# Small loads of the folded tables in another order, their users five and three steps later, and folds of batch 2 in other steps

## The chip, the cores and the metric

The kernel runs on one core of a Trainium2 chip. The metric is the device time of one execution in microseconds. Every time below is from runs on the chip or from the profile of one execution.

A core has engines that run side by side, each through its own list of instructions in order: PE (matrix multiplication into PSUM), DVE and POOL (element by element), ACT (functions and copies), and SP, which in this kernel only issues DMAs. An instruction that must wait for another engine or for a DMA holds up everything behind it on its own engine.

## The reference

A Fourier transform over sequence and features, of which the real part is kept, and then a gated feed-forward block:

```python
def _attn_ref(x):                                  # x: 8 x 3008 x 256
    X = np.fft.fft(x, axis=1)
    X = np.fft.fft(X, axis=2)
    return X.real.astype(np.float32)

def _moe_ref(x, w_gate, w_val, w_out):             # x: 24064 x 256, d_ff 1536
    gate = 1.0 / (1.0 + np.exp(-(x @ w_gate)))
    val = x @ w_val
    return (gate * val @ w_out).astype(np.float32)
```

## The kernel before

**Steps.** After a start-up, one loop runs 576 steps: 8 batches of 6 chunks of 12 steps (`i0` = 12, `per` = 72). A chunk is 252 output rows and their mirror images; a step is one slice of 128 of the 1536 hidden features. In step `i` PE multiplies `pk` (`front_a`) and `qk` (`front_b`) of the chunk into a PSUM bank, ACT and DVE make gate times value of step `i - 1` out of its bank (`gate_a`, `gate_b`), and PE multiplies older results with the output weights (`back`). Three PSUM banks rotate. A bank is started by ACT (`seed`, L851), which for step `i` must wait until the bank's previous use, step `i - 3`, is over: its last reader is `gate_b(i - 3)` (DVE L897), which stands in pass `i - 2` of the loop. `front_a` of step `i` waits for its `seed`.

**POOL.** Every three steps are a group. After the second and the third step of a group POOL makes seven and six sums of blocks of the hidden activations (L903, tile `sf`), which PE reads some three steps later (`po<-sf`).

**Closing a chunk.** `back` of the last group copies PSUM into the tile `c` in two steps, 3 and 4 after the start of the next chunk (`i % 12` of 3 and 4), and queues 24 small jobs in `later`: sums on `c` (DVE L987), transposes into `os` (DVE L995) and the stores (SP L1011, L1015). Each step takes two or three of them.

**Side work by hand.** Work for the next batch is put into steps by number: `at(i, f)` runs `f` at the end of step `i`; `gap[i]` runs it on DVE inside `gate_b`, just ahead of L897, in place of one job of `later`; `mid` puts matmuls between two steps. There is no scheduler: every engine has its instructions in the order in which these calls make them.

**Folds.** `fold_ops(b, 2)` gives the folds of batch `b` on POOL: six `point` (L550) and two small `first` (L554), six `across` (L563), three `feat` (L557, L558, L560, a trio), then seven more. `later_folds(b, s0)`, where `s0` is the first step of the batch before, spreads the first 17 over steps. For batch 2, `s0` is 72. In `gap[s0 + 18]` and on, `turn` (DVE L621) multiplies the folded data by tangents; the first two `turn` read what the second trio wrote, the next two need the third trio.

**Folded tables.** From batch 2 on a folded table is used. `table_rows` and `quarter_load` (SP L308) bring it into tiles named `st` in the profile. `quarter_small(i)` (eight DMAs each, one number per row and column) brings `self` (i = 0), `other` (i = 1; both L319) and `angle` (i = 2, L315), in steps 78, 79 and 80 (`per + 6 + i`). `quarter_ops` works on them: `turns` makes tangents of `angle` (L336 to L338), `eight` (L357) makes sums of the table, `ratios` uses `self` and `other` (L341 to L343), `cross` uses the table (L347 to L350). Five of these go into `gap`, in the order of the steps 83 to 87: `turns`, `eight(0)`, `eight(1)`, `ratios`, `cross`. `xr` copies for batch 3 (L156 to L169) go out on SP in steps 75 to 79 and 87 on.

**SP.** All these DMAs, the stores of the output and the loads of `ek` (L839) share SP's one queue, in order.

Of the kernel before, what the change touches and what calls it, by code (L numbers as in the profile page):

```python
# [81 lines left out]
def kernel(  # L82
# [216 lines left out]
    def quarter_src(g, par, t, cols):  # L299
        return (stab[0:TB, t, par:NQ:2, cols], rtab[par * TB : (par + 1) * TB, t, :, cols])[g]  # L300
# [10 lines left out]
    def quarter_small(i):  # L311
        for g, par, lo in TILES:
            if i == 2:
                for t in range(2):
                    nc.sync.dma_start(out=TAB["angle"][lo : lo + TB, t * N3 : (t + 1) * N3],  # L315
                                      in_=quarter_src(g, par, t, NE))
            else:
                for h, col in enumerate((0, NE)):
                    nc.sync.dma_start(out=TAB[("self", "other")[i]][lo : lo + TB, h * N3 : (h + 1) * N3],  # L319
                                      in_=quarter_src(g ^ i, par, 0, col))  # L320
# [772 lines left out]
    per = NFT * len(chunks)  # L1093
    side, mid, gap = {}, {}, {}

    def at(i, *fs):
        side.setdefault(i, []).extend(fs)
# [18 lines left out]
    i0 = NFT  # L1116
# [40 lines left out]
        at(per + 2 + i, lambda i=i: quarter_load(i // 2, i % 2))  # L1157

    for i in range(3):
        at(per + 6 + i, lambda i=i: quarter_small(i))  # L1160

    def make_tables():
        clear, between, sums, copies = quarter_ops()
        at(per + 7, clear)
        for i, f in zip((11, 12, 13, 14, 15), between, strict=True):
            gap[per + i] = [f]
        for i, f in zip((10, 19), sums):
            at(per + i, f)
        for i, f in zip((21, 23, 17, 19, 25, 27), copies, strict=True):
            at(per + i, f)  # L1170
    at(per + 5, make_tables)

    def later_folds(b, s0):

        ops = fold_ops(b, 2)
        slots = [i for i in range(s0 - (3 if b == 2 else i0), s0 + i0 + 5) if i % i0 < 5 or i < s0 and b == 2]
        for i, f in enumerate(ops[0:17]):
            at(slots[i * len(slots) // 17], f)
        for i, f in zip((24, 25, 26, 27, 28, 36, 37), ops[17:], strict=True):
            at(s0 + i, f)  # L1180
        for i, f in enumerate(TURN.pop(b)):
            gap[s0 + 18 + i] = [f]
        swaps, last, first = MORE.pop(b)
        at(s0 + 24, swaps[1])
        at(s0 + 39, swaps[0])
        for i, f in enumerate(first):
            gap[s0 + 28 + i] = [f]
        for i, f in enumerate(last):
            gap[s0 + 43 + i] = [f]
# [6 lines left out]
    for b in range(2, B):  # L1196
        s0 = (b - 1) * per
        at(s0 - 4 if b == 2 else s0 - i0 - 1, lambda b=b, s0=s0: later_folds(b, s0))
        at(s0 + 3 * i0 + 2, lambda b=b: seq_start(b))
        for blk in range(2):  # L1200
            mid[s0 + (4 - blk) * i0 + 5] = lambda b=b, blk=blk: quarter(b, blk)
        at(s0 + 4 * i0 + 5, lambda b=b, s0=s0: later_ends(b, s0))
        if b < B - 1:
            at(s0 + 4 * i0 + 6, lambda b=b: load_x(b + 1))
            for i, f in enumerate(mirror_x(b + 1)):
                at(list(calm(s0))[i // 2], f)
# [3 lines left out]
    for i in range(count):  # L1210
# [14 lines left out]
        between = gap.pop(i, [])  # L1225
        if not between and later and i < count - 8:
            between = [later.pop(0)]
# [75 lines left out]
```

## Time and profile before

| | us |
|---|---|
| median of 3 runs | 1921.85 (1921.27 to 1922.58) |
| the profiled execution | 1923.08 |
| its span, first to last instruction | 1921.3 |
| PE busy | 1900.5 (99%) |
| DVE busy | 1517.0 (79%) |
| ACT busy | 1353.3 (70%) |
| POOL busy | 1545.7 (80%) |

The page has, for each engine, the time in which it did something and that time's share of the span. PE is the engine that is nearly always busy. An average hides single stretches, so the other views matter: the waits (who waited for whom, total, times, longest), the timeline of an engine (start, length, engine, line, operation, output <- input, shape, count, and in brackets the idle time before it with what ended it), and tables of chosen stretches (busy time of each engine, instructions in brackets, then the granted clock of PE, the share of the DMA engines and GB/s). In a timeline, instructions of one line that follow each other are merged into one row, with their number at its end.

The mean granted clock of PE over the span is 0.997 of full speed.

The same lines of code in different batches can be told apart by time: batch 1's steps begin at 285.93 us (step 72), and steps there are about 3.1 us apart.

### The profile page before, as it was taken

What the parts mean: (1) busy time and instruction counts of PE and PEld (TensorE: products, weight loads), DVE (VectorE), ACT (ScalarE), POOL (GpSimd) and SP (SyncE); (2) the same over time, 40 slices, a digit from 0 to 9 for tenths busy, and PEclk for the clock granted to TensorE, in tenths of its full rate; (3) what the DMA queues carried; (4) which work ended last, traced back from release to release, by engine and by line L of the source; (5) the groups of instructions that cost most, each with busy time, mean ns of one, the idle gap of its engine ahead of it and who ended that gap; (6) DMA issues with size and microseconds to landing.
All of it is one profiled execution on the core that took longest, in us unless ns stands there. A gap on an engine that the chain in (4) does not pass through costs nothing.

```text
span 1921.3 us, 35824 instructions
## 1 busy us (share of the span) xinstructions
PE 1900.5 (99%) x11740; PEld 1760.8 (92%) x11740; DVE 1517.0 (79%) x3351; ACT 1353.3 (70%) x3219; POOL 1545.7 (80%) x2742
## 2 busy tenths in 40 slices
PE   8999998999999999999999999999999999999999
PEld 5799997999999999999999999999999999999998
DVE  7677875977978789787788877988788787976775
ACT  4876765777777777777777777777767777777775
POOL 2489967996999879997799877999789996877770
PEclk9999999999999999999999999999999999999999
DMA  8353234222023121221212123112120120011011
GB/s 313 110 97 72 65 105 96 64 52 79 16 48 73 34 80 21 63 54 31 86 34 60 39 38 87 39 47 50 34 80 14 31 45 15 15 23 19 15 17 30
DMA packets 198833, 110.05 MB, mean 57 GB/s; under 512 B 139269, under 2 KB 189168, under 8 KB 196856
## 3 DMA queue, kind: packets, MB, share of 16 engines
q1 hardware_dynamic: 198070, 107.25, 23.4%
q8 instruction: 94, 1.54, 0.3%
q14 instruction: 91, 0.75, 0.1%
q10 hardware_dynamic: 546, 0.51, 0.1%
q0 software_dynamic: 32, 0.00, 0.0%
HBM read 73.56 MB, written 47.87 MB: 63 GB/s over the span
## 4 chain that ended last, share of the span: by engine, by line
PE 95%; DMA 2%; SPq 1%; ACT 1%; DVE 0%; issue 0%; ACTq 0%; DVEq 0%
PE pf L134 50%; PE po L134 42%; PE sum L134 2%; DMA xr<-in_xf_dram 1%; DMA wf<-in_moe_w_out_dram 1%; SPq L433 1%; PE ps L134 1%; PE ev L134 0%; DMA st<-rtab 0%; SPq L221 0%; DMA raw<-in_moe_w_val_dram 0%; SPq L308 0%; PE pe L134 0%; SPq L164 0%; DVE z L881 0%
## 5 line engine op out<-in xcount | busy, mean ns | idle before, releaser
L903 POOL TENSOR_TENSOR sf<-h,sf 128x168 f32<-128x168 f32 (+1 forms) x1104 | 618.8, 581 | 71.0 <-DVE h L897 69.1
L903 POOL TENSOR_TENSOR sf<-h 128x168 f32<-128x168 f32 (+1 forms) x920 | 522.3, 587 | 180.0 <-DVE h L897 178.0
L134 PE MATMUL pf<-pk,G 128*128 128x252 f32 (+1 forms) x2304 | 583.6, 376 | 9.6 <-ACT pf L851 9.6
L134 PE MATMUL pf<-qk,G 128*128 128x252 f32 (+1 forms) x2304 | 583.6, 376 | 1.0 <-ACT ae L866 1.0
L851 ACT ACTIVATE pf<-ek,ge 128x252 f32<-128x252 f32 (+1 forms) x1142 | 538.3, 471 | 30.6 <-DVE h L897 10.9
L134 PE MATMUL po<-sf,wf 128*128 128x168 f32 (+1 forms) x2944 | 509.0, 306 | 0.0
L134 PEld LDWEIGHTS pf<-pk,G 128*128 128x128 f32 x2304 | 436.3, 190 | 63.3 <-ACT pf L851 10.6
L866 ACT ACTIVATE ae<-pf 128x504 f32<-128x504 f32 (+1 forms) x576 | 339.4, 589 | 219.5 <-PE pf L134 217.8
L134 PEld LDWEIGHTS po<-sf,wf 128*128 128x128 f32 x2944 | 454.4, 190 | 8.1
L897 DVE TENSOR_TENSOR h<-pf,z 128x252 f32<-128x252 f32 (+1 forms) x576 | 240.7, 418 | 279.3 <-ACT pf L894 276.3
L134 PE MATMUL po<-h,wf 128*128 128x168 f32 (+2 forms) x2584 | 460.9, 307 | 0.0
L987 DVE TENSOR_TENSOR c<-c 128x168 f32<-128x168 f32 (+1 forms) x920 | 451.4, 512 | 3.2
L881 DVE TENSOR_TENSOR z<-ae,pf 128x504 f32<-128x504 f32 (+1 forms) x576 | 385.0, 668 | 81.7 <-ACT h L880 77.5
L134 PEld LDWEIGHTS pf<-qk,G 128*128 128x128 f32 x2304 | 410.5, 190 | 32.7 <-ACT ae L866 2.2
L134 PEld LDWEIGHTS po<-h,wf 128*128 128x128 f32 x2584 | 410.5, 190 | 17.6 <-issue 0.9
L880 ACT ACTIVATE h<-pf 128x252 f32<-128x252 f32 (+1 forms) x576 | 217.4, 377 | 147.3 <-PE pf L134 132.1
L894 ACT ACTIVATE pf<-z 128x252 f32<-128x252 f32 (+1 forms) x576 | 214.2, 372 | 115.1 <-DVE h L893 112.3
L893 DVE TENSOR_TENSOR h<-h,pf 128x252 f32<-128x252 f32 (+1 forms) x576 | 233.3, 405 | 0.0
L903 POOL TENSOR_TENSOR sf<-sf 128x168 f32<-128x168 f32 (+1 forms) x184 | 101.4, 551 | 14.4
L903 POOL TENSOR_TENSOR sf<-sf,h 128x168 f32<-128x168 f32 (+1 forms) x184 | 108.6, 590 | 0.0
L970 ACT COPY c<-po 128x504 f32<-128x504 f32 (+1 forms) x138 | 78.5, 569 | 0.0
L995 DVE STREAM_TRANSPOSE os<-c 128x256 f32<-128x256 f32 x188 | 77.0, 428 | 0.4 <-issue 0.3
(166 smaller groups left out, 883.9 us busy)
## 6 DMA issues: line engine op xcount, KB each, us to landing
x<-xr SPq DMA_DIRECT2D x14, 1536.0 KB
out_dram<-os SPq DMA_DIRECT2D x368, 56.0 KB
xr<-in_xf_dram SPq DMA_DIRECT2D x90, 128.0 KB
x<-x SPq DMA_DIRECT2D x96, 96.0 KB
ek<-ed SPq DMA_DIRECT2D x40, 126.0 KB
xr<-in_xf_dram SPq DMA_DIRECT2D x12, 384.0 KB
out_dram<-os SPq DMA_DIRECT2D x284, 7.0 KB
x<-in_xf_dram SPq DMA_DIRECT2D x3, 1024.0 KB
```

What stands on the lines that cost most here:

```text
L134: nc.tensor.matmul(o, l, r, start=start, stop=stop, skip_group_check=True)
L851: nc.scalar.activation(PF[i][:, g], EK[i // NFT], AF.Copy, scale=ge[:, g, f : f + 1])
L866: nc.scalar.activation(AP[i], PF[i], AF.Copy, scale=2.0)
L880: nc.scalar.activation(H[p][:, fh, 0:n], PF[i][:, 0], AF.Sigmoid)
L881: nc.vector.tensor_tensor(z[:, :, ::-1], AP.pop(i), PF[i], op=ALU.subtract)
L893: nc.vector.tensor_tensor(h[:, fh, 0:n], h[:, fh, 0:n], pf[:, 1], op=ALU.mult)
L894: nc.scalar.activation(pf[:, 0], z[:, 0], AF.Sigmoid)
L897: nc.vector.tensor_tensor(h[:, fh, n:], pf[:, 0], z[:, 1], op=ALU.mult)
L903: nc.gpsimd.tensor_tensor(block(p, dst), block(p, a), block(p, b), op=(ALU.subtract, ALU.add)[op])
L970: (nc.vector.tensor_copy if t == 1 or t == 3 else nc.scalar.copy)(C[0][:, 3 * t * R : 3 * (t + 1) * R], PO[t][:, 0 : 3 * R])
L987: nc.vector.tensor_tensor(t[:, dst * R : (dst + 1) * R], *v, op=(ALU.subtract, ALU.add)[op])
L995: nc.vector.transpose(os_[0][:, s, 0:nb, h, :], t[:, c0 : c0 + nb * TB])
```

## The change

Two places of the hand-made order change; no instruction is added or removed.

1. `quarter_small` is called in the order 2, 0, 1 rather than 0, 1, 2: `angle` in step 78, `self` in 79, `other` in 80. `turns` moves from the gap of step 83 to that of step 88, and `ratios` from 86 to 89. `eight(0)`, `eight(1)` and `cross` stay in 84, 85 and 87.
2. The first 17 folds of batch 2 get steps written out by number. The six `point` and two `first` were in steps 69, 69, 70, 71, 72, 72, 73, 74 and are now in 69, 70, 71, 71, 72, 73, 74, 74 (`first` in 71 and 74, as before). The six `across` were in 75, 75, 76, 84, 85, 85 and are now in 83, 84, 84, 85, 86, 86. The three `feat` were in 86, 87, 88 and are now in 87, 88, 89. The other batches keep theirs.

```diff
     for i in range(3):
-        at(per + 6 + i, lambda i=i: quarter_small(i))
+        at(per + 6 + i, lambda i=i: quarter_small((2, 0, 1)[i]))
 
     def make_tables():
         clear, between, sums, copies = quarter_ops()
         at(per + 7, clear)
-        for i, f in zip((11, 12, 13, 14, 15), between, strict=True):
+        for i, f in zip((16, 12, 13, 17, 15), between, strict=True):
             gap[per + i] = [f]
...
     def later_folds(b, s0):
 
         ops = fold_ops(b, 2)
-        slots = [i for i in range(s0 - (3 if b == 2 else i0), s0 + i0 + 5) if i % i0 < 5 or i < s0 and b == 2]
-        for i, f in enumerate(ops[0:17]):
-            at(slots[i * len(slots) // 17], f)
+        calm_ = [i for i in range(s0 - i0, s0 + i0 + 5) if i % i0 < 5]
+        slots = [calm_[i * len(calm_) // 17] for i in range(17)]
+        if b == 2:
+            slots = [s0 + i for i in (-3, -2, -1, -1, 0, 1, 2, 2, 11, 12, 12, 13, 14, 14, 15, 16, 17)]
+        for i, f in zip(slots, ops):
+            at(i, f)
```

A step that has work in its `gap` takes its jobs of `later` behind `gate_b` instead, so those of steps 83, 86, 88 and 89 change places with the moved work; their number per step stays.

## The prediction

> **What bounds the kernel now.** I read the waits first, then PE's timeline around the longest of them, then the other engines' timelines there. PE is busy 1900.5 of 1921.3 us, so only the places where it stands still can be won, and the waits name one large one:
>
> ```profile
> DVE st L336 <- DMA st<-rtab: 12.2, 1, 12.2
> PE pf L134 <- ACT pf L851: 9.6, 1, 9.6
> ```
>
> One DVE instruction waits 12.2 us for small loads; one PE matmul waits 9.6 us for the ACT instruction that starts its PSUM bank. I call "step i" the pass of the main loop that begins on PE with the four matmuls `pf<-pk` of i; steps are 3.12 us apart wherever nothing is late (321.56 to 324.69). PE's timeline (start, length, engine, line, what, count, idle before):
>
> ```profile
> 307.26 1.12 PE L134 MATMUL pf<-qk,G 128*128 128x252 f32 x4 [0.31 <-ACT ae L866]
> 308.21 1.04 PE L134 MATMUL pf<-pk,G 128*128 128x252 f32 x4
> ...
> 311.21 1.12 PE L134 MATMUL pf<-qk,G 128*128 128x252 f32 x4 [0.54 <-ACT ae L866]
> 312.17 1.04 PE L134 MATMUL pf<-pk,G 128*128 128x252 f32 x4
> ...
> 324.69 1.01 PE L134 MATMUL pf<-pk,G 128*128 128x252 f32 x4
> ...
> 337.54 2.05 PE L134 MATMUL pf<-pk,G 128*128 128x252 f32 x4 [9.57 <-ACT pf L851]
> ...
> 342.51 1.01 PE L134 MATMUL pf<-pk,G 128*128 128x252 f32 x4
> ```
>
> Steps 79, 80, 84, 85 and 86 start at 308.21, 312.17, 324.69, 337.54 and 342.51. Step 85 comes 12.85 us after 84 instead of 3.12 (9.73 lost), 86 comes 4.97 after 85 (1.85 lost); 80 comes 3.96 after 79 (0.83 lost), and 79 3.70 after 78 at 304.51 (0.58 lost). The 1.85 us are the clock, in the table of stretches (the column before the DMA share is the granted clock):
>
> ```profile
> 328.00:330.80 2.80, 0.00 (x0) 0.00 (x0) 0.00 (x0) 0.00 (x0) 0.00 (x0) 1.00 0.11 14
> 330.90:341.10 10.20, 3.56 (x11) 3.21 (x12) 5.46 (x15) 3.06 (x7) 4.49 (x8) 0.50 0.27 46
> ```
>
> PE ended its last matmul at 327.97; some 2.9 us later the clock fell to 0.50, and stayed there 10.2 us, 3.56 of them busy. DVE:
>
> ```profile
> 306.80 2.25 DVE L987 TENSOR_TENSOR c<-c 128x164 f32<-128x164 f32 x2
> ...
> 322.77 0.41 DVE L893 TENSOR_TENSOR h<-h,pf 128x252 f32<-128x252 f32 x1
> 335.38 0.18 DVE L336 RECIPROCAL st<-st 128x3 f32<-128x3 f32 x1 [12.20 <-DMA st<-rtab]
> ...
> 357.50 0.78 DVE L621 SCALAR_TENSOR_TENSOR x<-x,st 128x256 f32<-128x256 f32 x1
> ```
>
> L336 stands in step 83 in front of L897, which ends step 83's use of a PSUM bank; L851 refills that bank for step 85. SP shows why it waits: its loads go out one after another, and `angle` (L315) is the last group.
>
> ```profile
> 316.34 2.19 SPq L319 DMA_DIRECT2D st<-in_stab_dram x4
> ...
> 331.96 2.30 SPq L315 DMA_DIRECT2D st<-rtab x4
> ```
>
> POOL has the folds:
>
> ```profile
> 304.87 3.99 POOL L563 TENSOR_TENSOR x<-x 128x512 f32<-128x512 f32 x3
> ...
> 343.41 3.74 POOL L563 TENSOR_TENSOR x<-x 128x512 f32<-128x512 f32 x3
> ...
> 356.55 0.72 POOL L560 TENSOR_TENSOR x<-x 128x254 f32<-128x254 f32 x1
> ```
>
> **The change, part by part.**
>
> *The loads.* Three groups of eight DMAs swap places on SP: `angle` takes the place that begins at 316.34, and the `self` and `other` groups move back by one, `other` to the place 330.03 to 334.27. Two pairs of `xr` copies keep their places between them; bytes and count are the same, so SP is free at the same time. The last landing released DVE at 335.35, 5.3 us after the first issue of its group (330.03). By that span `angle`, last issued at 322.08 in its new place, lands by 327.4 even if all 5.3 us follow the last issue; its use, now in step 88, stands where DVE is at 322.77 + 0.41 + 5 x 3.12 = 338.8: cover 11 us. `other` lands near 335.35; its use L342 is now in step 89, at 341.9, or 341.1 after the 0.8 us won below: cover 5.7 us. L357, which in the trace ran after the wait (338.2), now comes at step 84 near 325.5; its table loads were issued by 314.92, and the longest of that kind in the chain of waits landed 5.54 us after issue, so by 320.5. I cost all three waits at nothing. If a cover went, PE would lose the DVE wait less about 1.6 us (the bank's slack: L897 ended at 358.61 in step 90, its bank was needed at 361.26, and refilling takes 1.07, from 336.47 to 337.54). So -9.73 for the wait and -1.85 for the half clock: **-11.58**.
>
> *The three folds taken out of steps 75 and 76.* The L987 pair at 306.80 takes 2.25 us beside L563, and ends when that ends; step 80's 0.83 us follow from it: **-0.83**. The 0.58 of step 79 follow from an earlier pair (302.06, 3.04 us) that stood behind POOL's own sums until 304.87, and these stay: the sums end no sooner, since one L550 and the small L554 move ahead of the last six. Bounds -0.83 to -1.41; I take the first.
>
> *Where the folds go.* Steps 83 to 86 now carry six L563 (three before, in 84 and 85), and the three trios L557, L558, L560 move from steps 86, 87, 88 to 87, 88, 89. Let T0 be the end of step 83's L897, which releases POOL (336.47). From there POOL had no idle time until 358.86. The first L621 (step 90) needs the second trio, done at 356.55 + 0.72 = 357.27 = T0 + 20.8; DVE came at 357.50, 0.2 us later: no wait, and no room. Now three more L563, 3.74 / 3 = 1.25 each, stand in front of it: done at T0 + 24.55. L621 then holds up L897 behind it on DVE (357.50 to 358.61: 1.11) and the refill (1.07): step 92 starts at T0 + 26.7. Undisturbed, T0 would lie 0.15 after step 84's start (L894 of step 83 ended at 324.38, L897 takes 0.42 and a gap of 0.04), step 92 at T0 + 25.0 - 0.15 = 24.85. So PE waits **+1.9** at step 92. The third trio moves behind step 89's seven sums (358.82 to 362.90), to about T0 + 30.2; its reader (step 92) comes at 27.5 on the old rhythm, and with the 3.4 us by which DVE is late by then hardly waits. DVE runs these steps with little to spare, so I add **+0.3** for a second small wait at steps 93 or 94. POOL's sums of step 90 would be late too: PE reads the second at 366.38 (third `po<-sf` pair of step 93), POOL had it at 363.99; 3.75 later on the T0 scale it is short by 1.3, which the 1.9 at step 92 covers.
>
> The blocking seen at 306.80 can return, since the added folds lie beside L357 and L987: L987 takes 0.32 alone (at 309.88) and the pair there took 2.25. I count none of it separately: each such block is at most one L563 long (1.25), within the bank's slack of 1.6, and before L621 DVE waits 3.4 us anyway. Bounds for the moved folds together: 0 (POOL finds 3.75 us that it didn't use) to +2.9 (below the clock's fall).
>
> [...]
>
> *Ratios and tangents on DVE.* The same six instructions, in steps 88 and 89 rather than 83 and 86; L343 took 1.20 beside L563 and may again. They precede L621, so they lie within its wait: 0.
>
> Sum: -11.58 - 0.83 + 1.9 + 0.3 = -10.2. The profiled execution took 1923.08 us (span 1921.3 and 1.8 around it): 1912.9. The median of the runs is 1.23 lower: **1911.6**.
>
> **The rivals.**
>
> *No new wait.* POOL absorbs the folds: 1921.85 - 12.4 = 1909.4, or 1908.9 with step 79's loss gone. For it: three L563 fewer ahead of T0. Against: POOL idled at T0 already, so room before it is of no use after it, and it was full for 22 us.
>
> *The clock falls.* If the new wait reaches 2.9 us, the clock halves, and 10.2 us at half speed cost 5.1: 1909.4 + 2.9 + 5.1 = 1917.4. Against: 1.9 is 1.0 short, and 0.54 us at 311.21 did nothing to the clock.
>
> [...]
>
> *Slower.* One mechanism, POOL's lateness, hits twice: L621 waits at step 90 and again at step 92 (third trio), each long enough for the clock to fall. Price 2 x (2.9 + 5.1) = 16.0: 1909.4 + 16.0 = 1925.4. It decides where POOL is over 1 us later than reckoned at both. Against: at half clock PE leaves POOL 5 us, which fills the second wait.
>
> *The wait only moves.* Landings could slip with the `xr` copies between them, so that DVE waits at L342: it would need some 19 us of slip to eat the gain, and SP had sent everything by 334.27. Time about 1921.
>
> **How the numbers follow.** Forecast 0.62, no new wait 0.19, clock falls 0.10, slower 0.04, wait moves 0.05. About 0.2% (3.8 us) is what a measurement can tell from no change. The first two are faster, the third by 4.4 us mostly so: faster 0.91, same 0.05, slower 0.04. Range 1908.6 to 1916: from step 79's loss gone to a wait of 2.9 with part of a clock fall; the clock's full price and the last two rivals stay out.
>
> **What would show it.** Right: no idle before L336, L341 or L342; L315 ahead of both L319 groups; clock 1.00 from 324 to 400; the step after 311 on time while 307.26's 0.31 stays; a POOL wait of 1 to 3 us before the first L621, and PE idle once by 1 to 3 us about 25 us after step 84. Wrong: any DMA among DVE's waits after 300; L621 without a wait; PE waiting on `po<-sf`; a second stretch at 0.50.

## The result, and the profile after

| | before | after |
|---|---|---|
| median, us (5 runs each) | 1921.41 (1921.11 to 1922.58) | 1912.46 (1912.02 to 1912.84) |
| the profiled execution, us | 1923.08 | 1912.46 |
| its span, us | 1921.3 | 1910.7 |
| mean granted clock | 0.997 | 1.000 |

The ratio of the times is 0.9952, with a 95% interval of 0.9937 to 0.9967: faster by about 9 us. The forecast was 1911.6.

A measure used from here on is **PE's loss**: for each step from 79 to 108, the distance of its first `pf<-pk` matmul from that of the step before, less the undisturbed 3.125 us, summed over the steps that come more than 0.05 us late. Before it was 12.98 us (0.58 at step 79, 0.83 at 80, 9.73 at 85, 1.84 at 86). After it is 2.63: 0.61 at step 91, 1.04 at 92, 0.57 at 93 and 0.41 in small pieces up to 108. The difference, 10.35, is nearly the whole change of the span, 10.6. The span less the loss is between 1907.8 and 1908.7 us in all 14 profiles of this document, so losses can be compared from chip to chip within about half a us.

The waits of the kernel after (who waited for whom: total, times, longest). These are all the waits of PE's matmuls for ACT and the one wait of DVE's L621 for POOL; the 12.2 us of L336 are gone, and no DMA is among DVE's waits after 300 us:

```profile
PE pf L134 <- ACT ae L866: 0.8, 3, 0.3
DVE x L621 <- POOL x L560: 0.5, 1, 0.5
PE pf L134 <- ACT pf L851: 0.3, 1, 0.3
```

PE's timeline after, the first matmuls of steps 79, 80 and of 90 to 94:

```profile
307.85 1.01 PE L134 MATMUL pf<-pk,G 128*128 128x252 f32 x4
310.97 1.01 PE L134 MATMUL pf<-pk,G 128*128 128x252 f32 x4
...
342.22 1.01 PE L134 MATMUL pf<-pk,G 128*128 128x252 f32 x4
345.96 1.03 PE L134 MATMUL pf<-pk,G 128*128 128x252 f32 x4
350.12 1.12 PE L134 MATMUL pf<-pk,G 128*128 128x252 f32 x4 [0.29 <-ACT pf L851]
353.81 1.12 PE L134 MATMUL pf<-pk,G 128*128 128x252 f32 x4
357.04 1.01 PE L134 MATMUL pf<-pk,G 128*128 128x252 f32 x4
```

Steps 79 and 80 are 3.12 apart, and so is every step up to step 90 at 342.22. Then come 3.74, 4.16, 3.69 and 3.23. The loss is read from these starts, not from the brackets, since in the records the matmuls ahead end some 0.15 us behind the next start where nothing waits (308.86 against 308.69). The stretch in which the clock had been 0.50 is full (PE first, the granted clock before the DMA share):

```profile
330.90:341.10 10.20, 10.20 (x62) 9.66 (x62) 9.12 (x20) 8.69 (x20) 10.12 (x15) 1.00 0.44 66
```

SP sends `angle` first and `other` last:

```profile
316.54 1.89 SPq L315 DMA_DIRECT2D st<-in_stab_dram x4
...
331.12 1.87 SPq L319 DMA_DIRECT2D st<-in_stab_dram x4
```

DVE and POOL in the steps where the new loss arises:

```profile
304.96 1.24 DVE L987 TENSOR_TENSOR c<-c 128x164 f32<-128x164 f32 x2
...
339.01 1.27 DVE L338 TENSOR_SCALAR st<-st 128x3 f32<-128x3 f32 x1
...
343.32 0.38 DVE L342 TENSOR_TENSOR st<-st 128x6 f32<-128x6 f32 x1
...
347.98 0.74 DVE L621 SCALAR_TENSOR_TENSOR x<-x,st 128x256 f32<-128x256 f32 x1 [0.51 <-POOL x L560]
```

```profile
331.73 3.75 POOL L563 TENSOR_TENSOR x<-x 128x512 f32<-128x512 f32 x3
...
338.97 2.53 POOL L563 TENSOR_TENSOR x<-x 128x512 f32<-128x512 f32 x2
...
347.22 0.72 POOL L560 TENSOR_TENSOR x<-x 128x254 f32<-128x254 f32 x1
```

The second trio ends at 347.94 and releases the first L621 at 347.98. But DVE waited only 0.51 us for it: it had come late itself. From 336.7 to 347.4 it has hardly any idle time, and the moved work lies in there (L338, which works on 3 numbers per row, took 1.27 us beside an L563). So two engines arrive late together, and the profile alone doesn't tell which of them PE pays for. That is what most experiments ask.

### The profile page after: what moved, and what is told of

It reads as the page before. It is cut to its first block, busy times and chain, and to the rows that moved or that the text cites. A ratio compares the mean times of both kernels' runs of the same rounds, so it can differ in the third digit from the quotient of the medians.

```text
span 1910.7 us, 35839 instructions
## 1 busy us (share of the span) xinstructions
PE 1899.5 (99%) x11740; PEld 1759.9 (92%) x11740; DVE 1513.2 (79%) x3351; ACT 1351.7 (71%) x3219; POOL 1543.8 (81%) x2742
## 4 chain that ended last, share of the span: by engine, by line
PE 97%; DMA 1%; DVE 1%; ACT 1%; POOL 1%; issue 0%; SPq 0%; ACTq 0%; DVEq 0%; POOLq 0%
PE pf L134 51%; PE po L134 43%; PE sum L134 2%; DMA x<-in_xf_dram 1%; PE ps L134 1%; PE ev L134 1%; DMA raw<-in_moe_w_val_dram 0%; PE od L134 0%; POOL sf L903 0%; DVE z L881 0%; POOL x L563 0%; ACT ae L866 0%; PE pe L134 0%; DVE wf L451 0%; ACT wl L533 0%
## 5 line engine op out<-in xcount | busy, mean ns | idle before, releaser
L897 DVE TENSOR_TENSOR h<-pf,z 128x252 f32<-128x252 f32 (+1 forms) x576 | 240.7, 418 | 283.7 <-ACT pf L894 280.8
L987 DVE TENSOR_TENSOR c<-c 128x168 f32<-128x168 f32 (+1 forms) x920 | 443.1, 504 | 3.2
L893 DVE TENSOR_TENSOR h<-h,pf 128x252 f32<-128x252 f32 (+1 forms) x576 | 233.2, 405 | 0.0
```

The source lines that it names most:

```text
L893: nc.vector.tensor_tensor(h[:, fh, 0:n], h[:, fh, 0:n], pf[:, 1], op=ALU.mult)
L897: nc.vector.tensor_tensor(h[:, fh, n:], pf[:, 0], z[:, 1], op=ALU.mult)
L987: nc.vector.tensor_tensor(t[:, dst * R : (dst + 1) * R], *v, op=(ALU.subtract, ALU.add)[op])
```

## The experiments

Each edit is against the kernel after unless it says otherwise. Each comparison has its own runs of the kernel before, on the same chip; their medians were 1922.43 (old folds, folds alone, old load order, DVE relieved), 1923.07 (before again, load order alone, users elsewhere, two folds early), 1922.10 (both relieved, after again) and 1922.53 (the last two).

**Old folds.** The kernel after with the fold steps of before:

```diff
-        calm_ = [i for i in range(s0 - i0, s0 + i0 + 5) if i % i0 < 5]
-        slots = [calm_[i * len(calm_) // 17] for i in range(17)]
-        if b == 2:
-            slots = [s0 + i for i in (-3, -2, -1, -1, 0, 1, 2, 2, 11, 12, 12, 13, 14, 14, 15, 16, 17)]
-        for i, f in zip(slots, ops):
-            at(i, f)
+        slots = [i for i in range(s0 - (3 if b == 2 else i0), s0 + i0 + 5) if i % i0 < 5 or i < s0 and b == 2]
+        for i, f in enumerate(ops[0:17]):
+            at(slots[i * len(slots) // 17], f)
```

> The changed kernel with the folds of batch 2 back in their old steps; the load order and the new places of turns and ratios stay. PE's loss (what its steps 79 to 108 take over 3.12 us each) was 12.98 us before and 2.63 after. POOL theory (step 92 is late because the second trio ends late, three L563 more behind T0): no wait of L621 for POOL, nothing lost at steps 91 to 95, the 1.41 us of steps 79 and 80 come back; loss 1.4, median about 1911.3. DVE theory (DVE is late at L621 by itself, because turns and ratios now stand in steps 88 and 89): 1 to 2.6 us are still lost at 91 to 95, loss 2.4 to 4.0, median 1912.3 to 1913.9. Either way no wait of DVE for a DMA.

Measured: 1911.36 (1911.04 to 1911.47), ratio 0.9942 (0.9929 to 0.9954). Loss 1.46: 0.41 at step 91, 0.30 at 92, 0.65 at 93, 0.10 at 94; nothing at 79 and 80. DVE and POOL of this kernel:

```profile
346.64 0.78 DVE L621 SCALAR_TENSOR_TENSOR x<-x,st 128x256 f32<-128x256 f32 x1
```

```profile
345.69 0.73 POOL L560 TENSOR_TENSOR x<-x 128x254 f32<-128x254 f32 x1
```

The trio is done at 346.42, 23.06 after the end of step 83's L897 (T0, 323.36 here), and DVE starts L621 right behind L893, with no wait. So where nothing waits for POOL's trio 1.46 us remain, and these come from DVE's own lateness; the moved folds cost 2.63 - 1.46 = 1.2. Part of that lateness is POOL all the same: `cross`'s L349 takes 1.19 us here while POOL is in an L563, and took 0.47 before. The median is the one that the POOL theory gave, but by luck: its 1.4 us should have lain at steps 79 and 80, and they lie at 91 to 94. The trio moved by 1.27 (24.33 after), not by the 3.75 of three more L563: without the 12-us wait POOL comes to T0 with work left over, and starts the sums of step 83 at 324.95, 1.6 us behind T0 (in the kernel after it had idled 1.03 us and starts at 323.69). POOL at that place before, and with the old folds:

```profile
336.56 1.21 POOL L903 TENSOR_TENSOR sf<-h 128x168 f32<-128x168 f32 x2 [10.84 <-DVE h L897]
```

```profile
324.95 2.57 POOL L903 TENSOR_TENSOR sf<-h 128x168 f32<-128x168 f32 x4
```

**Folds alone.** The kernel before with the new fold steps (the edit is against before):

```diff
-        slots = [i for i in range(s0 - (3 if b == 2 else i0), s0 + i0 + 5) if i % i0 < 5 or i < s0 and b == 2]
...
+        if b == 2:
+            slots = [s0 + i for i in (-3, -2, -1, -1, 0, 1, 2, 2, 11, 12, 12, 13, 14, 14, 15, 16, 17)]
...
```

> The kernel before with only the folds of batch 2 moved; load order, turns and ratios as before. Both theories: L336 waits about 12 us for the angle loads, the clock falls, and the loss of steps 79 and 80 goes (0.83 by the prediction's step, 1.41 as the changed kernel showed). POOL theory: after the wait the second trio ends 3.75 us later than before, L621 waits for it by 3 us, step 92 is 1.7 to 1.9 late; median 1921.4 - 1.4 + 1.8 = 1921.8. DVE theory: with turns and ratios out of steps 88 and 89 nothing new is lost, 1920.0.

Measured: 1925.10 (1924.26 to 1927.40), ratio 1.0014 (1.0006 to 1.0023). The folds by themselves make the kernel slower, by 2.7 us in the medians. Both theories had put it lower, at 1921.8 and 1920.0. The profiled execution was the slowest of its runs (1927.40); its loss is 17.8, of which 11.11 at step 85, 1.58 at 86, 3.64 at 91 and 1.39 at 92. DVE, then POOL, ahead of step 91:

```profile
352.95 4.62 DVE L987 TENSOR_TENSOR c<-c 128x168 f32<-128x168 f32 x2
...
361.55 0.84 DVE L621 SCALAR_TENSOR_TENSOR x<-x,st 128x256 f32<-128x256 f32 x1
```

```profile
351.75 2.52 POOL L563 TENSOR_TENSOR x<-x 128x512 f32<-128x512 f32 x2
354.21 1.55 POOL L903 TENSOR_TENSOR sf<-h,sf 128x168 f32<-128x168 f32 x3
```

Two L987, 0.32 us each alone, take 4.62 and end at 357.57, right behind POOL's row of folds and sums (up to 357.38). PE then stood for 3.08 us and the clock fell for 3.41 us at 360.94: the rival of the falling clock, in an execution of this kernel. L621 doesn't wait for POOL here: the second trio is done at 360.52, and DVE comes later. Its other runs were not traced.

**Old load order.** The kernel after with `quarter_small(i)` as before:

```diff
-        at(per + 6 + i, lambda i=i: quarter_small((2, 0, 1)[i]))
+        at(per + 6 + i, lambda i=i: quarter_small(i))
```

> The changed kernel with self, other and angle loaded in the old order (angle last). By the landing seen before (335.35, 5.3 us after the first issue of its group) and L336 reached near 338 in step 88, angle is there in time without the new order: no wait of DVE for a DMA, median 1912.5 as the changed kernel. Rival, that the order is what removes the wait: L336 waits 1 to 3 us in step 88, PE loses 1 to 3 us more, 1913.5 to 1915.5.

Measured: 1912.38 (1911.77 to 1915.61), ratio 0.9951 (0.9937 to 0.9965), loss 2.58, no DMA wait. With the users in steps 88 and 89 the order of the loads makes no difference that can be measured here. This kernel differs from that of the old folds, on the same chip, by the folds and by that order, and is 1.0 us slower; the runs' ranges don't touch.

**DVE relieved.** `turns` in step 86, `ratios` in 88:

```diff
-        for i, f in zip((16, 12, 13, 17, 15), between, strict=True):
+        for i, f in zip((14, 12, 13, 16, 15), between, strict=True):
```

> The changed kernel with turns in step 86 instead of 88 and ratios in 88 instead of 89, so that DVE is less loaded just before the first L621; folds and load order as in the changed kernel. POOL theory: the second trio still ends about 24.3 us after T0, L621 waits for it longer (2 to 3 us instead of 0.5), step 92 is as late as before (1.6 us), some of the 1.0 us after it goes: median about 1912. DVE theory: the loss of steps 91 to 95 (2.4 us) falls below 0.5, median about 1910.3.

Measured: 1912.76 (1912.16 to 1916.51), ratio 0.9955 (0.9942 to 0.9967), loss 2.56 (0.66 at 90, 0.92 at 91, 0.57 at 93, the rest in small pieces). It relieved nothing: `ratios` now met the L563 that `turns` had met, and DVE came as late as before (its L893 of step 90 ended 23.82 after T0, against 23.86).

```profile
338.80 1.33 DVE L342 TENSOR_TENSOR st<-st 128x6 f32<-128x6 f32 x1
```

It can't tell the two engines apart.

**Before again.** The kernel before, unchanged, to see what of its loss recurs.

> The kernel before, profiled once more. The prediction took 0.83 us of steps 79 and 80 for a cost of the folds in steps 75 and 76. Theory of the fold: the pair of L987 in step 76 or 77 is held up again and steps 79 and 80 lose 1.4 us again. Theory of chance (the kernel with the old folds and the new loads lost nothing there, 0.0): the pair is held by POOL only when it comes at an unlucky moment, and this execution may lose nothing there. Both: the wait of 12 to 14 us at L336 and the half clock are there again, 11.5 to 13 us of PE.

Measured: 1922.01 in one run. Loss 11.85, all of it at steps 85 (10.21) and 86 (1.64). Nothing at 79 and 80: the 1.41 us that the profile of before shows there don't belong to every execution. That may be why its profiled execution stood 1.23 above the median; this run took 1.07 less than that execution and lost 1.13 less, which fits, but it ran on another chip.

**Load order alone.** The kernel before with only the new order of the loads (the edit is against before):

```diff
-        at(per + 6 + i, lambda i=i: quarter_small(i))
+        at(per + 6 + i, lambda i=i: quarter_small((2, 0, 1)[i]))
```

> The kernel before with only the load order changed (angle first); turns in step 83, ratios in 86, folds as before. angle's last DMA goes out near 321.5 and should land 1 to 1.5 us later, before L336 is reached near 322 to 323: little or no wait there. other's last goes out near 333 and lands near 334.5; L342 is reached near 331.5 in step 86: a wait of 2 to 4 us, less 1.6 of slack, so PE loses 1 to 2 us. Theory that the new order alone brings most of the gain: median 1911 to 1913. Rival, that only the later users bring it (small loads land some 5 us after their last issue): L336 still waits 4 us or more, 1914 to 1917.

Measured: 1913.69 (1912.94 to 1914.18), ratio 0.9951 (0.9938 to 0.9965), loss 4.35 (2.56 at step 88, 1.79 at 89). DVE and PE of it:

```profile
323.19 0.18 DVE L336 RECIPROCAL st<-st 128x3 f32<-128x3 f32 x1 [1.35 <-DMA st<-rtab]
...
335.35 1.15 DVE L342 TENSOR_TENSOR st<-st 128x6 f32<-128x6 f32 x1 [2.60 <-DMA out_dram<-os]
```

```profile
338.39 1.72 PE L134 MATMUL pf<-pk,G 128*128 128x252 f32 x4 [2.39 <-ACT pf L851]
```

`angle`, sent first, is only 1.35 us late for L336 in step 83, and 0.40 more for L337; PE loses nothing there. But `other` is now last, and `ratios` in step 86 waits for it: 2.60 us, put down to a store by the profile, although L342 reads no store; SP had sent the last of `other` at 333.65. So the order alone already removes the 12-us wait, and leaves 4.35 us in place of 2.63. Its ratio can't be told from that of the whole change (0.9952); by the losses it is 1.7 us behind. Most of the gain is to be had by either half of the change: an earlier `angle`, or later users.

**Users elsewhere.** Old folds, `turns` back in step 83, `ratios` in 88, `cross` in 86 (the edit is against old folds):

```diff
-        for i, f in zip((16, 12, 13, 17, 15), between, strict=True):
+        for i, f in zip((11, 12, 13, 16, 14), between, strict=True):
```

> Old folds, new load order, turns back in step 83, cross in 86, ratios in 88, so that nothing of them stands in 87 and 89. In the kernel with the old folds DVE came to the first L621 at T0 + 23.35, POOL's second trio ended at 23.06, and PE lost 1.46 us at steps 91 to 94. DVE theory for that kernel: DVE now comes before 22, POOL's trio at 23.06 becomes the bound, step 92 is 0.35 late instead of 0.7, and what follows shrinks: loss 0.3 to 0.7, median about 1910.4. Rival (the loss there is POOL's): loss stays near 1.4, median 1911.3.

Measured: 1911.91 (1911.38 to 1912.17), ratio 0.9942 (0.9929 to 0.9954). The loss is 2.01, but of other kinds: 0.56 and 0.82 at steps 79 and 80, as in the profile of before, and 0.63 at 88 and 89. At steps 91 to 94 nothing is left; DVE's L893 of step 90 ends 22.56 after T0, and it was 23.35 with old folds. The 0.63 at 88 and 89 come from `cross`, two of whose four instructions now take 1.2 us each beside an L563. So the loss at 91 to 94 seems to hang on where these small instructions stand, with the folds as they were. It is not shown cleanly: in this execution PE had stood 1.38 us at steps 79 and 80, POOL had caught up in that time (its trio ends 21.46 after T0, against 23.06 with old folds), and that may be part of why nothing is lost later. The standstill also brings DVE to L336 only at 323.09, 1.25 us later than in load order alone, and the loads are there by then.

**Two folds early.** The new folds, but two of the six L563 in steps 79 and 82:

```diff
-            slots = [s0 + i for i in (-3, -2, -1, -1, 0, 1, 2, 2, 11, 12, 12, 13, 14, 14, 15, 16, 17)]
+            slots = [s0 + i for i in (-3, -2, -1, -1, 0, 1, 2, 2, 7, 10, 12, 13, 13, 14, 15, 16, 17)]
```

> The changed kernel with two of its six moved L563 in steps 79 and 82 instead of 83 and 84, where POOL had idle time; turns in 88, ratios in 89 as in the changed kernel. POOL theory: the second trio ends 1 to 2.5 us earlier than T0 + 24.33, so DVE (T0 + 23.4 to 23.9) becomes the bound, and the loss falls from 2.6 to about 1.4, median about 1911.3. DVE theory: DVE is as late as in the changed kernel whatever POOL does, loss 2.4 to 2.6, median 1912.4. A loss at steps 80 to 86 would be a new one, from L987 beside the two folds.

Measured: 1911.56 (1911.32 to 1911.74), ratio 0.9940 (0.9927 to 0.9954), loss 1.76 (1.12 at 92, 0.54 at 93, 0.10 at 94). The trio comes 22.71 after T0, DVE still 23.82: DVE is the later one now, and the loss is near that of old folds.

**Both relieved.** Two folds early, the trios one step earlier, and `turns` in 87, `ratios` in 88, `cross` in 83:

```diff
-        for i, f in zip((16, 12, 13, 17, 15), between, strict=True):
+        for i, f in zip((15, 12, 13, 16, 11), between, strict=True):
...
-            slots = [s0 + i for i in (-3, -2, -1, -1, 0, 1, 2, 2, 11, 12, 12, 13, 14, 14, 15, 16, 17)]
+            slots = [s0 + i for i in (-3, -2, -1, -1, 0, 1, 2, 2, 7, 10, 12, 13, 13, 14, 14, 15, 16)]
```

> Two L563 in steps 79 and 82, the other four in 84, 85, 85 and 86, the trios in 86, 87, 88; cross in step 83, turns in 87, ratios in 88, nothing in 89; angle first. Both theories at once: POOL's second trio should end by T0 + 22.7 and DVE reach the first L621 at about T0 + 22, so step 92 (T0 + 24.85 without loss, L621's start + 2.14 otherwise) loses nothing: loss of steps 79 to 108 under 0.5 (2.63 in the changed kernel), 1.5 to 2.1 us faster than the changed kernel beside it. If the loss stays over 1.2, a third cause holds steps 91 to 94.

Measured: 1911.39 (1910.93 to 1912.09), ratio 0.9945 (0.9931 to 0.9958), loss 2.03 (0.59 at 79, 0.59 at 92, 0.75 at 93, 0.10 at 94). DVE:

```profile
302.19 3.05 DVE L987 TENSOR_TENSOR c<-c 128x164 f32<-128x164 f32 x2
...
347.24 0.97 DVE L621 SCALAR_TENSOR_TENSOR x<-x,st 128x256 f32<-128x256 f32 x1 [1.66 <-POOL x L560]
```

Here DVE comes early and waits 1.66 us for POOL, the kind of wait that the prediction drew for the kernel after. The expected loss under 0.5 was missed: 1.44 are lost at 92 to 94. T0 is no fixed mark in this kernel, since `cross` stands in front of it: it lies 1.19 us behind the start of step 84, and 0.14 in the kernel after. Counted from the start of step 84, DVE's L893 of step 90 ends at 21.57 (24.00 in the kernel after), and POOL's trio at 23.20 (24.47 in the kernel after, 22.85 in two folds early, 23.20 in old folds). So DVE was relieved, POOL was no earlier than with the old folds, and its trio is what holds step 92. The first line is the blocked pair of step 76 once more: with no L563 behind it, 0.59 us at step 79 stay and step 80 loses nothing.

**After again.** The kernel after, unchanged, on the chip of the last one.

> The changed kernel once more, on the same chip as the version above. Loss 2.6 at steps 91 to 108 again, nothing at 79 and 80 (the blocked pair was seen in 2 of 5 profiles with the old folds and in none of 5 with the new), no DMA among DVE's waits there, L621 waiting about 0.5 us for POOL.

Measured: 1913.47 (1913.17 to 1916.18), ratio 0.9960 (0.9947 to 0.9972); loss 2.66 at the same steps, L621 waits 0.5 again. Both relieved is 2.1 us faster beside it. Two of the five runs took 1915.57 and 1916.18 us, and their mean granted clock is 0.999 where the others have 1.000: 3.41 us at half clock in 1913 would make just that. So the clock seems to fall in some executions of the kernel after too (and in two of the five of DVE relieved, with 0.999 and 0.998). None of these was traced, so what lets it fall there stays open.

**Turns later.** The three places that put `turn` and its companions into `gap` one step later for batch 2, so that POOL has 3.1 us more:

```diff
-            gap[s0 + 18 + i] = [f]
+            gap[s0 + 18 + (b == 2) + i] = [f]
...
-        at(s0 + 24, swaps[1])
+        at(s0 + 24 + (b == 2), swaps[1])
...
-            gap[s0 + 28 + i] = [f]
+            gap[s0 + 28 + (b == 2) + i] = [f]
```

> The changed kernel with only the six turns of batch 2 one step later (91 to 96; the swap behind them and the six products that need it one step later too). POOL and the small operations as in the changed kernel. If step 92 is late because L621 waits for the second trio (T0 + 24.3): L621 now comes near T0 + 24 to 26.5, waits nothing for POOL, step 90 is free for DVE to catch up, and the loss of steps 91 to 95 falls from 2.6 to under 1; median 1 to 2 us under the changed kernel on the same chip. If DVE's lateness from turns and ratios in 88 and 89 alone sets it: step 91's 0.6 stays and about 1.5 us are lost in all, 1 us under the changed kernel. If neither: loss 2.6.

Measured: 1912.50 (1912.45 to 1912.79), ratio 0.9947 (0.9934 to 0.9961). The loss is 2.98, where under 1 was expected: 0.58 at 91, 0.59 at 92, 0.19 at 94, 1.07 at 95, 0.55 at 104 and 105. L621 doesn't wait; another reader of POOL does, on ACT:

```profile
357.71 0.68 ACT L376 ACTIVATE st<-st 128x570 f32<-128x570 f32 x1 [1.53 <-POOL st L353]
```

So POOL's lateness isn't used up by moving one reader: it is paid at the next, 1.07 at step 95. The 1.17 at steps 91 and 92 stay without any wait for POOL's results: they are DVE's. The 0.55 at 104 and 105 appears only in the two versions with later turns; its cause stays open.

**Turns later, folds early.** The last one with the fold steps of both relieved (the edit is against turns later):

```diff
-            slots = [s0 + i for i in (-3, -2, -1, -1, 0, 1, 2, 2, 11, 12, 12, 13, 14, 14, 15, 16, 17)]
+            slots = [s0 + i for i in (-3, -2, -1, -1, 0, 1, 2, 2, 7, 10, 12, 13, 13, 14, 14, 15, 16)]
```

> The same with two of the moved L563 in steps 79 and 82 and the trios in 86, 87, 88. POOL ends the second trio near T0 + 22, two us before it is needed; DVE has step 90 free. Loss of steps 79 to 108 under 0.5 unless the blocked pair of step 76 comes up (0.6), 2 us or more under the changed kernel on the same chip.

Measured: 1910.97 (1910.54 to 1911.28), ratio 0.9939 (0.9927 to 0.9951); loss 1.50 (0.41 at 91, 0.60 at 92, 0.49 at 104 and 105). Under 0.5 was expected and missed again: the 1.01 at 91 and 92 lie ahead of the first L621 and are DVE's, and the piece at 104 is there as before. The wait at L376 and the 1.07 at step 95 are gone with the early folds, and on the same chip the time falls by 1.5 us. It is the fastest kernel of the study; it was compared with the kernel after only through their runs of before, and those intervals overlap.

## Why the prediction came out right, point by point

The forecast of -10.2 stands against -10.6 between the two profiled executions and -9.0 between the medians. The main term was right. The other two were off in that pair of profiles, -0.83 for -1.41 and +2.2 for +2.63, and the two misses partly cancel, which is luck. Two of the prediction's own signs came out otherwise: L621 waits 0.51 us for POOL, not 1 to 3, and PE's loss is spread over steps 91 to 93 (0.61, 1.04, 0.57) rather than laid in one place.

**The wait and the half clock (-11.58): right.** Both are gone, and nothing took their place in steps 83 to 86. Three covers were named: `angle`, `other` and the table. None was used up. The 11 us of cover for `angle` were even too cautious: in load order alone its last piece was there at 323.76, where the prediction allowed it until 327.4.

**Steps 79 and 80 (-0.83): the mechanism was right as far as is seen, its frequency wrong.** In the profiled pair of executions the whole 1.41 us vanished; the prediction kept 0.58. But before again lost nothing there with the old folds. In 14 profiles the pair of step 76 was blocked for about 3 us in three: before, users elsewhere, both relieved. Of these the two with old folds lost 0.58 + 0.83 and 0.56 + 0.82, the one with moved folds 0.59 alone. So the moved folds take the 0.83 away when the block happens, by that one case. The prediction counted a chance event as a certain gain. It also carried the 1.23 between profiled execution and median over to the kernel after, whose profiled execution is its median (1912.46): the forecast for the profiled execution (1912.9) was nearer than that for the median.

**The moved folds (+1.9 at step 92, +0.3 behind): the sum was about right, its parts were not.** Measured: 1.65 up to step 92 and 0.98 behind it, 2.63 against 2.2. Several pieces hold: the second trio ended 24.33 us after T0 (predicted 24.55), the third 29.94 (30.2), and step 92 began 26.51 after it (26.7). Two steps failed.

The first: "DVE waits 3.4 us anyway" before L621, so that ratios and tangents cost 0. DVE was expected there 21.1 after T0 and came at 23.86; the wait was 0.51. `turns`, `ratios` and the pairs of L987 between them filled what had been thought free. Old folds and turns later put a price on it: 1.46 us and, at steps 91 and 92, 1.17 are lost with no wait for POOL's results, and with the users elsewhere those steps lose nothing (0.63 comes at 88 and 89 instead, and PE had stood at 79 and 80). A cost of 0 for an edit under another wait was the mis-sized term. It went unseen in the total, presumably because two engines that are late at the same place cost PE the later of the two, not both: relieving POOL alone (two folds early) left 1.76, and with DVE early (both relieved) 1.44 were left.

The second: the three added L563 were put at 3.75 us on the trio. Old folds shows 23.06 with the old steps, so 1.27. The 20.8 of the trace of before was measured behind a 12-us pause of POOL's supplier, in which POOL had caught up; the baseline went away with the wait. The sum 24.55 was near the measured 24.33 by luck: baseline and addition were wrong by about the same, in opposite directions. In time the folds cost 1.0 on one chip (old load order against old folds), and 1.2 in the loss.

A premise beside it doesn't hold either: that each block of DVE by POOL is at most one L563 long (1.25). In folds alone a single L987 took 4.00 us, and already in the trace of before the first of the pair at 302.06 took 2.42, with no L563 beside it. In these steps of the kernel after the longest L987 took 1.40 us (at 326.89), so this premise cost the forecast nothing.

**The rivals.** *No new wait* (1908.9 to 1909.4): no version tried came to it. *The clock falls*: not in the two profiles of the kernel after, though two runs of after again (0.999) look like it; in the profiles of folds alone, and of load order alone, it did. Its price of 5.1 us was too high: a fall after a short wait lasted one stretch of 3.41 us and cost 1.79 at step 89 there. *Slower by two waits*: no; behind step 92 the kernel after loses only 0.57 and smaller pieces, and the clock stays at 1.00. *The wait only moves*: not after, yet it is what happens with the load order alone, where L342 waits 2.60. There the mechanism needed no slip of 19 us, because the user stayed where it was.

**What brought the gain.** By the experiments: moving the two users is enough to end the wait (old load order 1912.38; the users alone, with the old folds too, were not run); the load order alone gives most of it (1913.69); the new fold steps give none and cost about 1.0 with the rest and 2.7 alone. In the one profile of folds alone the extra loss follows a long block of L987, with no wait of L621 for POOL; whether the same makes up the 2.7 of the medians was not traced.

## What to carry to other kernels

When a long wait goes, every margin measured behind it goes too: engines that had caught up during the wait are late again, and slack has to be counted from an undisturbed stretch. An edit laid under another engine's wait is free only up to the length of that wait as it will be, so add up the engine's own work to that point first. A stall in one profile that hangs on two engines meeting within tenths of a microsecond should be looked for in a second execution before it is put into a sum.

## What was not expected of the hardware

**A DVE instruction was held over several POOL instructions in a row.** The L987 of before beside which POOL did nothing took 0.33 us (median of 38), and pairs of them beside POOL's sums 0.94, 1.12 and 1.31 (at 339.55, 312.99 and 318.50). Small ones are hit as well: L338 took 0.17 us in users elsewhere, and 1.27 in the kernel after, beside one L563 of 1.29. But in three profiles the first of a pair ended only right behind a pause of POOL: in folds alone the pair took 4.62 us, over two L563 and several sums. The first of the pair, 4.00 us long, ended at 356.95, right behind POOL's first pause since the L563, 0.08 us at 356.76. The first of the pair in before ended at 304.48, with the same pause of 0.08 at 304.29, and in both relieved at 304.62, with it at 304.44. So these three ran on beside more than one instruction of POOL; why, no trace shows.

**How little idle time let the clock fall.** In every fall of the four executions that had one in this part, the time from the clock's first rise was a whole number of spans of 3.413 us: before 94 (rise at 10.01 us, fall at 330.87: 320.86 / 94 = 3.413), load order alone 96 (11.09, 338.77), folds alone 94 and 103. What goes with a fall is how little PE did in the last such span. Load order alone, before and after the fall; then two folds early and folds alone near its end, two spans of their grids after which the clock didn't fall (columns as above):

```profile
335.36:338.77 3.41, 1.02 (x6) 0.58 (x5) 3.31 (x8) 1.38 (x4) 3.41 (x6) 1.00 0.53 82
338.77:342.18 3.41, 3.41 (x13) 3.16 (x12) 2.75 (x7) 2.40 (x6) 3.33 (x9) 0.50 0.48 81
```

```profile
346.50:349.91 3.41, 2.64 (x15) 2.12 (x15) 3.41 (x8) 2.05 (x5) 3.41 (x7) 1.00 0.28 98
```

```profile
1920.83:1924.24 3.41, 1.66 (x8) 1.13 (x6) 0.42 (x1) 0.37 (x1) 0.00 (x0) 1.00 0.40 125
```

PE was busy for 1.02 of 3.41 us, and the clock fell; with 2.64 and with 1.66 it did not. The span ahead of the fall in before, 327.45 to 330.87, had 0.53. Over all spans of the grids of the 14 profiles, up to the ends of the kernels, the two kinds don't mix: at full clock, each of the ten spans with up to 1.05 us of work was followed by half clock, and each with 1.66 or more by full clock. The 1.02 us in load order alone, 30% of the span, lie around one pause of 2.39 us, and that was enough for a fall. So the "2.9 us later" that the prediction read from the trace of before was where that span happened to end, not a threshold; its price of a wait, and its upper bound of 2.9 us without a fall, rested on that. The falls also differed in length: in load order alone PE was busy for all of the next span, and the fall lasted that one span (3.41 us); in before PE was busy for 0.00 and 0.16 us of the next two, and it lasted three (10.24).
